# Down weights converted later, their loads behind an activation store, and a reordered, halved last token block

## The chip, the core and the metric

The kernel runs on one core of a Trainium2 chip. The metric is the device time of one execution in microseconds (us); lower is better. Five executions of the kernel before gave 632.99 to 637.2 us, median 633.97.

## What is computed

Linear attention with decay (4 batches, 8 heads, 768 tokens of 64 values, blocks of 64 tokens with a carried state), then a feed-forward block on its output. With `x` the attention output, 3072 tokens x 512:

```python
h = x @ w_in                      # 512 x 2048
g = np.maximum(0.01 * h, h)
out = g @ w_out                   # 2048 x 512, float32
```

`w_in` and `w_out` arrive as 64-bit floats, so each weight has to be turned into 32 bits on the chip. All products are wanted at nearly full float32 precision.

## The kernel before

The 3072 tokens are 24 chunks of 128 (`NCH`), in 6 groups of 4 chunks (`NG`, `GC`; 512 tokens a group). The 2048 hidden columns are 8 pieces of 256 (`NP`). The work has three parts that overlap.

*Attention*, one round for each chunk (`round_of`): transposes of k and q (L319), small 64x64 products (L274) into the PSUM tiles `po` and `psc`, and copies and products on VectorE, ScalarE and GpSimd. A round's last products (`inter(1)`) wait until a tiny copy has read `po` (L402). Each round also issues the loads of q, k (L299) and v (L304) for the chunk after the next. Its result is split in three reduced-precision parts: `xh` (L418), `xl` (L419), `xm` (L421).

*Up* (`up(g, p)`): for a group g and piece p, two halves of 128 hidden columns. Each half is three products of four 128x512 matmuls (L544): xh*wh and xl*wl summed in `b10` or `b11`, and xm*wm in `b2`. ScalarE evacuates the first sum to `t` (L565), VectorE joins it with `b2` in `gs` (L569), ScalarE applies the leaky ReLU (Prelu, L571), and SP stores the 512 KB to a DRAM tile `g` (L574). A step takes 24 matmuls.

*Down* (`down_load`, `down(g, p)`): SP loads `g` back (L584), ScalarE and VectorE split it in three (L591 to L594), and TensorE multiplies with the three parts of the down weights (L607). For every token block `tb` of 128 tokens there are two accumulators, `acc[tb][0]` for the h and l products and `acc[tb][1]` for the m products ("summed differences"). For tb = 3 both lie in the one PSUM tile `po`, for tb = 2 in `psc`; the other blocks have two separate tiles. After the last piece ScalarE reads `acc[tb][0]` into `t` (L616), VectorE joins it with `acc[tb][1]` (L618), and SP stores 256 KB of output (L621).

*Weights.* `to_float32` turns half a piece from 64 to 32 bits: SP loads 512 KB to one of two `raw` buffers (L470 for up, L473 for down weights), ScalarE does three operations (L482, L484, L486), VectorE two (L488, L489). For the down weights, `w_out(p)` does both halves and SP stores the result, 512 KB, in a DRAM tile `wo` (L523), because the space in which down weights end up is still taken by attention. Later `w_out_parts(p)` loads it (L527) and splits it in three.

*Order.* No order is written by hand. A list `seq` gives the pieces of work in rank; the `Plan` books each operation on an engine with a cost in us and emits the operation that can start first by its own clock; rank only breaks ties. A DMA is booked as busy for its cost, and what needs it may start 2.0 us later. Every engine then runs its own list strictly in the order in which the plan emitted it, SP's DMA issues among them. An operation without reads may go as soon as its buffer is free: the raw loads (`add("DMA", 1.6, load, [], ...)`) are such, so they may be emitted long before the place of their piece in `seq`. In `seq` a conversion `("wo", n_out)` follows every second step of the up work of groups 2 to 5, from step 0 on:

```python
        if n_out < NP and n % 2 == 0:
            seq.append(("wo", n_out))
            n_out += 1
```

Of the kernel before, what the change touches and what calls it, by code (L numbers as in the profile page):

```python
# [15 lines left out]
ALU = mybir.AluOpType  # L16
# [12 lines left out]
WS = S * U  # L29
# [7 lines left out]
class Plan:  # L37
# [20 lines left out]
    def add(self, eng, us, fn, reads=(), writes=(), rank=0.0):  # L58

        n, deps = len(self.ops), set()  # L60
        for k in reads:
            w, r = self.last.setdefault(k, [None, []])
            if w is not None:
                deps.add(w)
            r.append(n)
        for k in writes:
            w, r = self.last.setdefault(k, [None, []])
            if w is not None:
                deps.add(w)
            deps.update(r)  # L70
            self.last[k] = [n, []]
        deps.discard(n)
        ways = {eng: us} if isinstance(eng, str) else dict(zip(eng, us))
        if self.chain is not None:
            self.chains[self.chain].append(n)
        self.ops.append((ways, fn, deps, (self.rank + rank, n), set(writes)))
# [76 lines left out]
def kernel(  # L153
# [10 lines left out]
    nc = tc.nc  # L164
# [5 lines left out]
    d_model, d_ff = moe_w_in.shape  # L170
    KO = d_model // P
    NP = d_ff // (2 * P)
    NCH = B * NCB
    GC = 4
    NG = NCH // GC
# [12 lines left out]
    def sb(shape, name, dt=F32):  # L188
        return pool.tile(shape, dt, name=name, tag=name)
# [12 lines left out]
    raw = [sb([P, 2 * d_model], f"raw{i}") for i in range(2)]  # L202
    lows = [sb([P, d_model], f"low{i}", I32) for i in range(2)]
    w32 = sb([P, 2, d_model], "w32")
    tt = [sb([P, T], f"t{i}") for i in range(2)]
    gs = [sb([P, 2, T], f"gs{i}") for i in range(2)]
    WO = [dram.tile([P, 2 * d_model], F32, name=f"wo{p}", tag=f"wo{p}") for p in range(NP)]
    G = [[dram.tile([P, 2 * T], F32, name=f"g{g}_{p}", tag=f"g{g}_{p}") for p in range(NP)] for g in range(NG)]
# [38 lines left out]
    add = plan.add  # L247
# [209 lines left out]
    w_in_r = moe_w_in.rearrange("(ko ki) n -> ki ko n", ki=P)  # L457
    n_raw = 0

    def to_float32(kind, p, h, dst, key):  # L460

        nonlocal n_raw
        j, n_raw = n_raw % 2, n_raw + 1
        r, low, kl = raw[j], lows[j], f"low{j}"
        d = dst.bitcast(I32)

        def load():
            r64 = r.bitcast(I64)
            if kind == "wi":
                nc.sync.dma_start(out=r64.rearrange("p (k f) -> p k f", k=2),  # L470
                                  in_=w_in_r[:, 2 * h:2 * h + 2, p * 2 * P:(p + 1) * 2 * P])
            else:
                nc.sync.dma_start(out=r64, in_=moe_w_out[(2 * p + h) * P:(2 * p + h + 1) * P, :])  # L473

        def words(i, dt):
            return r.bitcast(dt).rearrange("p (n two) -> p n two", two=2)[:, :, i]

        def addend(dt, i):
            return low.bitcast(dt).rearrange("p (n two) -> p n two", two=2)[:, :, i]

        add("DMA", 1.6, load, [], [f"raw{j}"])
        add("ACT", 0.67, lambda: nc.scalar.activation(out=dst, in_=words(1, F32), func=AF.Abs, scale=2.0 ** -110),  # L482
            [f"raw{j}"], [key])
        add("ACT", 0.78, lambda: nc.scalar.activation(out=addend(U16, 0), in_=words(0, U32), func=AF.Copy, bias=0.0, scale=2.0 ** -29),  # L484
            [f"raw{j}"], [kl])
        add("ACT", 0.77, lambda: nc.scalar.activation(out=addend(F16, 1), in_=words(1, F32), func=AF.Copy, bias=0.0, scale=2.0 ** -100),  # L486
            [f"raw{j}"], [kl])
        add("DVE", 0.42, lambda: nc.vector.tensor_scalar(d, d, 3, None, op0=ALU.logical_shift_left), [], [key])  # L488
        add("DVE", 1.0, lambda: nc.vector.tensor_tensor(d, d, low, op=ALU.add), [kl], [key])  # L489
# [21 lines left out]
    def w_in(p):  # L511
        for h in range(2):
            to_float32("wi", p, h, w32[:, h, :], f"w32{h}")
        parts(p, w32f, ["w320", "w321"])

    ATT = ["fk", "fq", "sc"] + [f"{x}{i}" for x in ("k", "q", "v", "kT", "qT", "qsT") for i in range(2)] + [f"st{i}" for i in range(4)]
    NR = 4
    graw = [att[:, j * 2 * T:(j + 1) * 2 * T] for j in range(NR)]

    def w_out(p):  # L520
        for h in range(2):
            to_float32("wo", p, h, w32[:, h, :], f"w32{h}")
        add("DMA", 1.5, lambda: nc.sync.dma_start(out=WO[p], in_=w32f), ["w320", "w321"], [f"WO{p}"])  # L523

    def w_out_parts(p):
        j = p % NR
        add("DMA", 1.5, lambda: nc.sync.dma_start(out=graw[j], in_=WO[p]), [f"WO{p}"], [f"gr{j}"], rank=-3.0)  # L527
        parts(p, graw[j], [f"gr{j}"])
# [5 lines left out]
    def up(g, p, half=None):  # L534
# [42 lines left out]
    acc = [[b1[0], b2], [b1[1], pt.rearrange("p y t -> p (y t)")]] + [  # L577
        [z[:, i].rearrange("p y t -> p (y t)") for i in range(2)] for z in (psc, po)]
    ACC = [["b10", "b2"], ["b11", "pt"], ["psc", "psc"], ["po", "po"]]
# [17 lines left out]
    def down(g, p):  # L597

        nonlocal n_t
        for tb in range(GC):  # L600
            for pp in (p, p + 1):
                j = (g * NP + pp) % NR

                def go(tb=tb, pp=pp, j=j):
                    for f in range(2):
                        for z in range(3):
                            nc.tensor.matmul(acc[tb][z // 2], lhsT=ring[j][z][:, f * T + tb * P:f * T + (tb + 1) * P],  # L607
                                             rhs=W[pp][z][:, f * d_model:(f + 1) * d_model],
                                             start=pp == 0 and f == 0 and z != 1, stop=pp == NP - 1 and f == 1,
                                             skip_group_check=True)  # L610

                add("PE", 1.36, go, [f"r{z}{j}" for z in "hlm"] + [f"w{z}{pp}" for z in "hlm"], sorted(set(ACC[tb])))
            if p + 2 == NP:
                jt, n_t = n_t % 2, n_t + 1
                t, y = tt[jt], gs[jt][:, 0, :]
                add("ACT", 0.6, lambda t=t, tb=tb: nc.scalar.activation(out=t, in_=acc[tb][0], func=AF.Copy, bias=0.0, scale=(1.0 + 1.0 / S) / U),  # L616
                    [ACC[tb][0]], [f"t{jt}"], rank=-1.5)
                add("DVE", 0.69, lambda t=t, y=y, tb=tb: nc.vector.scalar_tensor_tensor(y, acc[tb][1], -1.0 / WS, t, op0=ALU.mult, op1=ALU.add),  # L618
                    [f"t{jt}", ACC[tb][1]], [f"gs{jt}"], rank=-1.5)
                rows = out[(g * GC + tb) * P:(g * GC + tb + 1) * P, :]  # L620
                add("DMA", 0.8, lambda rows=rows, y=y: nc.sync.dma_start(out=rows, in_=y), [f"gs{jt}"], [], rank=-1.5)  # L621

# [3 lines left out]
    seq = [("a", 0), ("wi", 0), ("a", 1), ("a", 2), ("up", 0, 0, 0), ("a", 3), ("wi", 1), ("up", 0, 1, 0), ("b", 4),  # L626
# [4 lines left out]
    nxt, n_out = 3 * GC, 0  # L631
    steps = [(g, p) for g in range(2, NG) for p in range(NP)]
    for n, (g, p) in enumerate(steps):
        while nxt < (g + 1) * GC:
            seq.append(("r", nxt))
            nxt += 1
        seq.append(("up", g, p))
        if nxt < NCH and nxt // GC < g + 2:
            seq.append(("r", nxt))
            nxt += 1  # L640
        if n_out < NP and n % 2 == 0:
            seq.append(("wo", n_out))
            n_out += 1
        if g == NG - 1:
            seq.append(("wp", p))
# [5 lines left out]
    for n, x in enumerate(seq):  # L651
        plan.rank = float(n)
        if x[0] in "abr":
            {"a": alone, "b": begun, "r": round_of}[x[0]](x[1])
        elif x[0] == "wi":
            w_in(x[1])
        elif x[0] == "up":
            up(*x[1:])
        elif x[0] == "wo":
            w_out(x[1])  # L660
        elif x[0] == "wp":
            if not freed:
                add("DVE", 0.0, lambda: None, [], ATT + [f"gr{j}" for j in range(NR)])
                freed = True
            w_out_parts(x[1])
        elif x[0] == "dl":
            plan.rank = n - 8.0
            down_load(*x[1:])
        else:
            down(*x[1:])  # L670
# [31 lines left out]
```

## Time and profile before

| | |
|---|---|
| profiled execution | 633.97 us |
| its span, first to last instruction | 632.2 us |
| median of five executions | 633.97 us |
| TensorE busy (PE) | 615.3 us |
| VectorE (DVE) / ScalarE (ACT) / GpSimd (POOL) busy | 350.4 / 277.9 / 80.4 us |
| mean granted TensorE clock | 0.996 |
| raw loads of down weights, first and last start | 95.6 and 186.3 us |
| raw loads of down weights, issue to landing | 3.5 to 6.0 us |
| store of a converted down weight, median to landing | 3.9 us |
| first and last load of a converted down weight (L527) | 293.9 and 344.8 us |

PE is TensorE's matmul side, PEld its weight loads. A line such as "PE po L274 <- issue: 3.5, 2, 2.0" in a list of waits gives the engine, the tile and line of the instruction that waited, what ended the wait, the total, the number of waits and the longest (us); "issue" means that the profile shows nothing the engine waited for. In a list in order of time a line gives start, duration, engine, line, operation, output and inputs, shape and count, and in brackets the idle time before it with what ended it. In a table of stretches each row gives start and end, length, the busy time of PE, PEld, DVE, ACT and POOL, the granted TensorE clock, the mean busy share of the 16 DMA engines, and GB/s.

### The profile page before, as it was taken

How to read it: one execution, taken by the hardware profiler on the slowest of the kernel's cores; microseconds unless marked ns; L12 is line 12 of the kernel's file. 1: busy time of each engine (PE TensorE's matmuls, PEld its weight loads, DVE VectorE, ACT ScalarE, POOL GpSimd, SP SyncE). 2: the span in 40 equal slices, each digit the busy share in tenths (PEclk: the TensorE clock that was granted, in tenths of full speed). 3: DMA queues.
4: the chain of work that ended last, by engine and by line, in shares of the span. 5: the costliest groups of instructions: out<-in, count | busy, mean ns of one | idle time of the engine just before them, and what ended most of it. 6: DMA issues, size and time to landing. Idle time of an engine off the chain costs nothing.

```text
span 632.2 us, 13360 instructions
## 1 busy us (share of the span) xinstructions
PE 615.3 (97%) x5587; PEld 515.0 (81%) x5587; DVE 350.4 (55%) x475; ACT 277.9 (44%) x403; POOL 80.4 (13%) x91
## 2 busy tenths in 40 slices
PE   7899999999989999999999999999999999999997
PEld 6787888887868888888888888888888888888885
DVE  5987986565754245245348866553735554545531
ACT  5687778766656444443344442312312222313111
POOL 3443500232331123021000000000000000000000
PEclk9999999999989999999999999999999999999999
DMA  7978857796986356233525663341432423343201
GB/s 194 248 213 213 242 198 252 265 261 219 268 240 203 107 144 169 100 102 119 200 117 185 219 212 134 116 150 67 160 108 101 167 87 132 116 132 116 85 0 67
DMA packets 103693, 101.54 MB, mean 161 GB/s; under 512 B 78545, under 2 KB 80593, under 8 KB 103633
## 3 DMA queue, kind: packets, MB, share of 16 engines
q1 hardware_dynamic: 103488, 100.68, 50.2%
q8 instruction: 44, 0.72, 0.5%
q14 instruction: 17, 0.13, 0.1%
q10 hardware_dynamic: 144, 0.00, 0.0%
HBM read 65.02 MB, written 35.65 MB: 159 GB/s over the span
## 4 chain that ended last, share of the span: by engine, by line
PE 89%; DMA 4%; DVE 2%; issue 2%; ACT 1%; SPq 1%; ACTq 0%
PE b L544 39%; PE b L607 17%; PE po L607 10%; PE psc L607 10%; PE po L274 4%; PE pt L607 3%; PE psc L274 3%; DMA raw<-in_moe_w_in_dram 3%; PE po L319 1%; PE pt L319 1%; SPq L299 1%; DMA att<-in_v_dram 1%; DMA att<-g 1%; DVE gs L569 0%; DVE xl L419 0%
## 5 line engine op out<-in xcount | busy, mean ns | idle before, releaser
L569 DVE SCALAR_TENSOR_TENSOR gs<-b,t 128x512 f32<-128x512 f32 x96 | 66.1, 689 | 90.7 <-PE b L544 72.2
L591 ACT ACTIVATE xh<-att 128x1024 fp32r<-128x1024 f32 x48 | 50.9, 1061 | 141.8 <-PE po L607 138.3
L592 DVE SCALAR_TENSOR_TENSOR xl<-att,xh 128x1024 fp32r<-128x1024 f32 x48 | 58.7, 1222 | 95.7 <-ACT xh L591 95.6
L544 PE MATMUL b<-xh,wh 128*128 128x512 f32 (+1 forms) x416 | 107.5, 380 | 1.1 <-ACT xh L418 0.8
L544 PE MATMUL b<-xl,wl 128*128 128x512 f32 (+1 forms) x416 | 105.6, 376 | 0.5 <-DVE wl L500 0.5
L544 PE MATMUL b<-xm,wm 128*128 128x512 f32 (+1 forms) x416 | 104.8, 376 | 0.8 <-DVE gs L569 0.6
L565 ACT ACTIVATE t<-b 128x512 f32<-128x512 f32 x96 | 57.0, 594 | 70.4 <-PE b L544 69.8
L544 PEld LDWEIGHTS b<-xl,wl 128*128 128x128 f32 x416 | 75.2, 189 | 14.9 <-DVE wl L500 0.7
L544 PEld LDWEIGHTS b<-xh,wh 128*128 128x128 f32 x416 | 74.2, 189 | 16.0 <-ACT xh L418 1.2
L544 PEld LDWEIGHTS b<-xm,wm 128*128 128x128 f32 x416 | 73.8, 188 | 15.7 <-DVE gs L569 1.4
L607 PE MATMUL b<-wh,xh 128*128 128x512 f32 x192 | 74.8, 390 | 0.1
L607 PE MATMUL b<-wl,xl 128*128 128x512 f32 x192 | 74.7, 389 | 0.0
L571 ACT ACTIVATE gs<-gs 128x1024 f32<-128x1024 f32 (+1 forms) x52 | 51.6, 992 | 41.4 <-DVE gs L569 41.0
L594 DVE SCALAR_TENSOR_TENSOR xm<-xl,xh 128x1024 fp32r<-128x1024 f32 x48 | 58.7, 1225 | 4.6
L332 POOL TENSOR_TENSOR att<-att 128x512 f32<-128x512 f32 (+1 forms) x24 | 26.2, 1092 | 143.4 <-PE po L319 131.7
L607 PEld LDWEIGHTS b<-wh,xh 128*128 128x128 f32 x192 | 36.1, 188 | 8.0 <-ACT t L565 0.5
L607 PEld LDWEIGHTS b<-wl,xl 128*128 128x128 f32 x192 | 36.1, 188 | 7.3
L274 PE MATMUL po<-att 64*64 64x64 f32 x1472 | 33.6, 222 | 4.1 <-issue 3.5
L607 PE MATMUL pt<-wm,xm 128*128 128x512 f32 x96 | 37.4, 389 | 0.0
L607 PE MATMUL psc<-wh,xh 128*128 128x512 f32 x96 | 37.3, 389 | 0.0
L607 PE MATMUL psc<-wl,xl 128*128 128x512 f32 x96 | 37.3, 389 | 0.0
L607 PE MATMUL psc<-wm,xm 128*128 128x512 f32 x96 | 37.3, 389 | 0.0
(69 smaller groups left out, 818.4 us busy)
## 6 DMA issues: line engine op xcount, KB each, us to landing
att<-g SPq DMA_DIRECT2D x48, 512.0 KB, 3.2
g<-gs SPq DMA_DIRECT2D x44, 512.0 KB, 3.0
raw<-in_moe_w_in_dram SPq DMA_DIRECT2D x16, 512.0 KB, 4.8
raw<-in_moe_w_out_dram SPq DMA_DIRECT2D x16, 512.0 KB, 4.5
att<-in_k_dram SPq DMA_DIRECT2D x48, 128.0 KB, 4.2
att<-in_q_dram SPq DMA_DIRECT2D x48, 128.0 KB, 3.6
att<-in_v_dram SPq DMA_DIRECT2D x24, 256.0 KB, 4.5
out_dram<-gs SPq DMA_DIRECT2D x24, 256.0 KB, 2.1
```

The source lines that it names most:

```text
L274: nc.tensor.matmul(dst[HALF[cols]], lhsT=lhsT[HALF[rows]], rhs=rhs[HALF[rows]], start=start, stop=True, skip_group_check=True)
L299: nc.sync.dma_start(out=dst[:, z * HP:(z + 1) * HP, :], in_=y[z::2].rearrange("h p d -> p h d"))
L319: nc.tensor.transpose(out=at[y], in_=src[:, 2 * y:2 * y + 2, :].rearrange("p a d -> p (a d)"), identity=ident)
L332: add("POOL", 1.15, lambda: nc.gpsimd.tensor_tensor(kr[nr], kr[nr], _bc(pow_k, 3, D)[nr], op=ALU.mult), ["fk"], [f"k{i}"])
L544: nc.tensor.matmul(dst, lhsT=w[z][:, kk * 2 * P + f * P:kk * 2 * P + (f + 1) * P], rhs=x[z][:, kk, toks], start=start and kk == 0, stop=kk ...
L565: add("ACT", 0.6, lambda t=t, b=b: nc.scalar.activation(out=t, in_=b, func=AF.Copy, bias=0.0, scale=(1.0 + 1.0 / S) / U), [kb], [f"t{jt}"] ...
L569: add("DVE", 0.69, lambda t=t, r=r: nc.vector.scalar_tensor_tensor(r, b2, -1.0 / WS, t, op0=ALU.mult, op1=ALU.add), [f"t{jt}", "b2"], [f"g ...
L571: add("ACT", 1.05 if half is None else 0.6, lambda: nc.scalar.activation(out=y, in_=y, func=AF.Prelu, bias=0.0, scale=1.0, alpha=0.01), [] ...
L591: add("ACT", 1.05, lambda: nc.scalar.activation(out=h, in_=graw[j], func=AF.Copy, bias=0.0, scale=NEAR), reads, wr("h"))
L592: add("DVE", 1.25, lambda: nc.vector.scalar_tensor_tensor(l, graw[j], 1.0, h.bitcast(F32), op0=ALU.mult, op1=ALU.subtract), reads + [f"rh{ ...
L594: add("DVE", 1.25, lambda: nc.vector.scalar_tensor_tensor(m, l.bitcast(F32), -S, h.bitcast(F32), op0=ALU.mult, op1=ALU.add), [f"rh{j}", f" ...
L607: nc.tensor.matmul(acc[tb][z // 2], lhsT=ring[j][z][:, f * T + tb * P:f * T + (tb + 1) * P], rhs=W[pp][z][:, f * d_model:(f + 1) * d_model ...
```

## The change

Two edits to the down weights' conversion. It starts after step 4 of the up work of group 2 and later instead of step 0 (still every second step, eight in all), and its raw loads now read the key of the activation store of the step before (`G` of that group and piece), so that they can't be issued before that store has landed. And an edit to the last token block of the kernel (group 5, tb = 3): the 8 matmuls of h and l of both last pieces come first, then the 4 of m, instead of h, l, m in turn; the joining operation on VectorE and the output store are done in two halves of 256 columns. All other token blocks keep their order; the PE operations are only booked in the plan with costs written in another way.

```diff
-    def to_float32(kind, p, h, dst, key):
+    def to_float32(kind, p, h, dst, key, after=()):
...
-        add("DMA", 1.6, load, [], [f"raw{j}"])
+        add("DMA", 1.6, load, after, [f"raw{j}"])
...
-    def w_out(p):
+    def w_out(p, after):
         for h in range(2):
-            to_float32("wo", p, h, w32[:, h, :], f"w32{h}")
+            to_float32("wo", p, h, w32[:, h, :], f"w32{h}", after)
...
+            done = p + 2 == NP
+            very_last = done and g == NG - 1 and tb == GC - 1
...
+            for pps, zs in (((p, p + 1), (0, 1)), ((p, p + 1), (2,))) if very_last else (((p,), (0, 1, 2)), ((p + 1,), (0, 1, 2))):
+                add("PE", 0.227 * 2 * len(pps) * len(zs), lambda pps=pps, zs=zs, go=go: go(pps, zs),
+                    needs(pps, ["hlm"[z] for z in zs]), sorted({ACC[tb][z // 2] for z in zs}))
...
-                add("DVE", 0.69, lambda t=t, y=y, tb=tb: nc.vector.scalar_tensor_tensor(y, acc[tb][1], -1.0 / WS, t, op0=ALU.mult, op1=ALU.add),
-                    [f"t{jt}", ACC[tb][1]], [f"gs{jt}"], rank=-1.5)
...
-                add("DMA", 0.8, lambda rows=rows, y=y: nc.sync.dma_start(out=rows, in_=y), [f"gs{jt}"], [], rank=-1.5)
+                n = 2 if very_last else 1
+                for i in range(n):
+                    cols = slice(i * d_model // n, (i + 1) * d_model // n)
+                    add("DVE", 0.69 / n + 0.08 * (n - 1),
+                        lambda t=t, y=y, tb=tb, cols=cols: nc.vector.scalar_tensor_tensor(
+                            y[:, cols], acc[tb][1][:, cols], -1.0 / WS, t[:, cols], op0=ALU.mult, op1=ALU.add),
+                        [f"t{jt}", ACC[tb][1]], [f"gs{jt}{i}" if n == 2 else f"gs{jt}"], rank=-1.5)
+                    add("DMA", 0.8 / n, lambda rows=rows, y=y, cols=cols: nc.sync.dma_start(out=rows[:, cols], in_=y[:, cols]),
+                        [f"gs{jt}{i}" if n == 2 else f"gs{jt}"], [], rank=-1.5)
...
-        if n_out < NP and n % 2 == 0:
-            seq.append(("wo", n_out))
+        if n_out < NP and n >= 4 and n % 2 == 0:
+            seq.append(("wo", n_out, ["G%d%d" % steps[n - 1]]))
             n_out += 1
```

More of the change, by code (lines that the diff above doesn't have):

```diff
@@ L600, in down, with go @@
         for tb in range(GC):
-            for pp in (p, p + 1):
-                j = (g * NP + pp) % NR
-                def go(tb=tb, pp=pp, j=j):
+            done = p + 2 == NP
+            very_last = done and g == NG - 1 and tb == GC - 1
+            def go(pps, zs, tb=tb):
+                for pp in pps:
+                    j = (g * NP + pp) % NR
                     for f in range(2):
-                        for z in range(3):
+                        for z in zs:
                             nc.tensor.matmul(acc[tb][z // 2], lhsT=ring[j][z][:, f * T + tb * P:f * T + (tb + 1) * P],
@@ L610, in go, with needs @@
                                              skip_group_check=True)
-                add("PE", 1.36, go, [f"r{z}{j}" for z in "hlm"] + [f"w{z}{pp}" for z in "hlm"], sorted(set(ACC[tb])))
-            if p + 2 == NP:
+            def needs(pps, zs):
+                return [f"{x}{z}{y}" for pp in pps for z in zs for x, y in (("r", (g * NP + pp) % NR), ("w", pp))]
+            for pps, zs in (((p, p + 1), (0, 1)), ((p, p + 1), (2,))) if very_last else (((p,), (0, 1, 2)), ((p + 1,), (0, 1, 2))):
+                add("PE", 0.227 * 2 * len(pps) * len(zs), lambda pps=pps, zs=zs, go=go: go(pps, zs),
+                    needs(pps, ["hlm"[z] for z in zs]), sorted({ACC[tb][z // 2] for z in zs}))
+            if done:
                 jt, n_t = n_t % 2, n_t + 1
@@ L659 @@
         elif x[0] == "wo":
-            w_out(x[1])
+            w_out(*x[1:])
         elif x[0] == "wp":
```

## Prediction

> **What bounds the kernel now.** I read the page first (busy shares, slices), then what TensorE waited for, then the busy time in stretches of 20 and of 2 us, then TensorE in order of time around its stalls, and the last 5 us.
>
> ```profile
> PE 615.3 (97%) x5587; PEld 515.0 (81%) x5587; DVE 350.4 (55%) x475; ACT 277.9 (44%) x403; POOL 80.4 (13%) x91
> q8 instruction: 44, 0.72, 0.5%
> ```
>
> TensorE is busy 615.3 of 632.2 us and has the same matmuls after the change, so only its 16.9 us of gaps, and time at a lower clock, can be won. The rows below are stretches: length, then busy PE, PEld, DVE, ACT, POOL, granted clock, DMA share, GB/s.
>
> ```profile
> 140.00:160.00 20.00, 18.45 (x306) 15.71 (x303) 11.49 (x19) 12.98 (x22) 4.75 (x6) 1.00 0.74 233
> 160.00:180.00 20.00, 17.88 (x320) 14.82 (x319) 12.42 (x22) 14.03 (x23) 7.12 (x8) 1.00 0.95 270
> 180.00:200.00 20.00, 19.54 (x203) 16.23 (x204) 9.94 (x19) 13.01 (x21) 6.05 (x7) 0.91 0.69 211
> ...
> 240.00:260.00 20.00, 20.00 (x212) 16.81 (x211) 8.20 (x15) 8.45 (x13) 4.49 (x6) 1.00 0.47 121
> ```
>
> From 80 to 140 us TensorE is full. In 140 to 200 it idles 1.55 + 2.12 + 0.46 = 4.13 us; from 200 to 300, where attention goes on and no down weight is converted, 0.04. Its waits in 138 to 186 us (total, times, longest):
>
> ```profile
> PE po L274 <- issue: 3.5, 2, 2.0
> PE b L544 <- DVE gs L569: 0.6, 1, 0.6
> ```
>
> The big one waits for nothing that the profile shows. TensorE in order of time, at both places:
>
> ```profile
> 141.52 0.28 PE L274 MATMUL po<-att 64*64 64x64 f32 x3
> 143.35 0.45 PE L274 MATMUL po<-att 64*64 64x64 f32 x13 [1.55 <-issue]
> ...
> 178.09 0.41 PE L274 MATMUL po<-att 64*64 64x64 f32 x13
> 180.47 0.42 PE L274 MATMUL po<-att 64*64 64x64 f32 x3 [1.97 <-issue]
> 180.82 2.08 PE L544 MATMUL b<-xh,wh 128*128 128x512 f32 x4
> 182.69 1.68 PE L544 MATMUL b<-xl,wl 128*128 128x512 f32 x4
> 184.21 0.62 PE L544 MATMUL b<-xm,wm 128*128 128x512 f32 x2
> ```
>
> Both stops are inside a group of 16 products (after 3, after 13), so no operand is missing: instructions are. Counting a weight load and a matmul for each record, the first stop is at instruction 4,289 of TensorE's program and the second at 5,314: 1,025 apart, four times 256 and one. After the second, 8 matmuls take 184.21 - 180.82 = 3.39 us instead of 8 x 0.2275 = 1.82: 1.57 us lost to the clock.
>
> ```profile
> 180.00:182.00 2.00, 1.53 (x6) 1.22 (x7) 0.00 (x0) 1.07 (x3) 0.96 (x1) 0.64 1.07 325
> 182.00:184.00 2.00, 2.00 (x7) 1.52 (x6) 1.71 (x3) 0.59 (x1) 1.04 (x3) 0.51 0.89 199
> ```
>
> [...] 0.72 MB in 44 packets is 16.4 KB each, 11,226 instructions / 256 = 43.9; [...] the stop of 1.55 us brought no drop. [...] Output stores of 256 KB land in 2.0 to 3.1 us (median 2.1)[...].
>
> **The change, part by part.**
>
> *Conversions leave 95 to 202 us.* Each of the eight has two loads and one store of 512 KB, on ScalarE 2 x (0.666 + 0.788 + 0.780) = 4.47 us, on VectorE 2 x (0.51 + 0.74) = 2.5 us. All go past SP's q, k, v loads and activation stores; GpSimd has none of it. TensorE's order stays up to the round at 139 us; later third products move by a place or two and rounds spread out from one per step to one per two steps. What goes: the stops, 1.55 + 1.97; the clock, 1.57; the wait on gs and its neighbour, 4.13 - 3.52 = 0.61. Sum 5.70 us.
> What hides fetches elsewhere is length: in steady matmuls a block lasts 128 x 0.2275 = 29 us. Only a block that lies wholly in an attention round is short. In before there are three: at 139 us (3.4 us by its durations), 176 us (2.5 us) and 283 us (2.7 us). The first two stopped: their next block came 5.4 and 4.5 us after they began. The third didn't, with a DMA share of 0.34. So a fetch takes under 2.7 us in quiet and 4.5 to 5.4 us in traffic. In after, by the order of its program: the block at 139 us is the same (traffic less by the store of w and two loads: I take 0.2 us, ends 0 and 1.5); the next has ten instructions of up matmuls in it, 2.9 us (I take 0); the one in the round of chunk 21, about 280 us, is now 2.1 us, and conversions run there: with a fetch of 3.3 us, between quiet and traffic, it stops 1.2 us (ends 0 and 3.2, and 1.57 for the clock).
>
> *They arrive at about 195 to 302 us.* From 200 to 300 ScalarE was busy 42.3 of 100 us, VectorE 41.3; plus 8 x 4.47 and 8 x 2.5 makes 78 and 61. DMA share there was 0.42 on average; 12.6 MB more in 100 us, by 419 GB/s at a share of 1.06 (138 to 140 us), adds 0.31: 0.73, below the 0.74 to 0.95 that hurt. Nothing saturates. Their last consumer, the load at L527 of the eighth weight at 344.8 us, comes 40 us later.
>
> *The wait.* Each pair of raw loads waits on SP for the landing of an activation store: 2.6 us in quiet, 5.3 at most there (200 to 300 us). Behind it on SP are q, k, v loads of the next round and the next store. That store is a step away, 24 x 0.2275 = 5.5 us, so it isn't late; q, k, v are late by up to 3 us, but rounds are now about 14 us apart, so nobody waits: 0. The raws land 3.5 (quiet) to 6.0 us after issue. The planner books 1.5 + 2.0 and 1.6 + 2.0 = 7.1 us for the two, reality takes 6.1 + 0.7 of issue in quiet. ScalarE and VectorE take the conversion in order; behind a late raw stand L565 (t), L402 (which lets a round's last products go) and L569 (which frees b2). Following the two programs with these durations against TensorE's products of 0.91 us, six of the eight conversions leave 0.2 to 1.8 us of slack; the one beside the round of chunk 21 leaves none, the last one misses by 0.5. The last, to show it: its raws are in ScalarE's reach 0.1 + 0.3 + 2.6 + 0.35 + 3.5 = 6.9 us after the Prelu of step (4, 1) ends; in ScalarE's order 4.47 of conversion, two evacuations (0.6 each), a Prelu (1.06) and an attention copy (0.6) follow before t of step (4, 4) is out, 14.2 in all; TensorE wants that buffer 15 products and two short groups, 13.7, later. I take 0.5 + 0.4 for raws that land later than in quiet, 0.9 us (ends 0 and 8 x 1.2).
>
> *The tail.*
>
> ```profile
> 627.78 0.60 ACT L616 ACTIVATE t<-po 128x512 f32<-128x512 f32 x1 [2.12 <-PE po L607]
> 628.41 0.69 DVE L618 SCALAR_TENSOR_TENSOR gs<-po,t 128x512 f32<-128x512 f32 x1 [2.03 <-ACT t L616]
> ```
>
> The summed products (h, l) now end four matmuls, 0.91 us, before the last; that could cover the 0.60 of the activation. But po is one tile with both sums, and in the program as built that activation still waits for the last matmul of po. So 0 (if it didn't: -0.6). The halves: 2 x 0.41 (the 128x256 row of L370 takes 0.41) instead of 0.69 ends VectorE 0.13 later; [...] the first half's issue, 0.34, fits beside the second. Net -0.1 (-0.3 to +0.2).
>
> **Sum.** The profiled execution took 633.97 us, 1.8 more than its span, and is also the median of the five (632.99 to 637.2). 633.97 - 5.70 = 628.27; + 0.2 + 1.2 + 0.9 - 0.1 = 630.5.
>
> **Rivals.**
> *Nothing new stops* (0.15): quiet fetches below 2.1 us and all slack holds: 628.2. For it: 0.04 us idle from 200 to 300 us; against: more traffic there.
> *The stop only moves* (0.28): the short block at 280 us meets full traffic (3.0 us, then the clock, 1.57), and the one at 139 us keeps 1.0: 628.27 + 3.0 + 1.57 + 1.0 + 0.9 - 0.1 = 634.6. For it: that block is the shortest of all; against: traffic of 0.73, not 0.95.
> *The waiting loads hold ScalarE up* (0.09, slower): one mechanism, at L482 behind the raw: if store and raw land as in traffic (5.3 + 6.0 instead of 6.1), the pair is 4 us over the booked 7.1, TensorE idles what exceeds some 1 us of slack, 8 x 1.5 = 12: 628.2 + 12 = 640. It decides from about 2.2 us over (8 x 1.2 = 9.6: 637.9). Against: G stores of 2.6 us in quiet.
> *The likeliest* (0.48): 630.5, its own range 629.0 to 632.0.
>
> **Numbers.** 0.5% is 3.2 us, about what a measurement of this kernel can tell from no change: faster is below 630.8. The likeliest case lies on that side with somewhat over two thirds: 0.15 + 0.35 = 0.50 faster; 0.41 same; 0.09 slower. Range 628.0 to 635.0: it leaves out the slow case and the upper third of the moving stop.
>
> **What would show it.** Right: no "issue" wait over 0.3 us and clock 1.00 in 120 to 200 us; PE 20.00 in those stretches; ScalarE near 0.78 in 200 to 300; one stop of TensorE near 280 us at most; the last activation still after the last matmul. Wrong: "issue" of over 1 us at 139 us (then its traffic was stores and q, k, v), waits of ScalarE on raw of over 1 us each with TensorE idle behind L565 or L402, or a tail shorter by 0.6.

## The result and the profile after

The changed kernel took 630.92 us (median of 22 runs, 627.2 to 635.24); the kernel before, run beside it, 634.07 us (43 runs, 630.75 to 637.95). The ratio is 0.9947, with a 95% interval of 0.9929 to 0.9965: about 3.4 us won, and somewhere between 2.2 and 4.5. The forecast of 630.5 us was met. Single runs of one kernel lie up to 8 us apart, more than the effect, so each trace below is one sample: the medians say how much, the traces say where.

The profiled execution of the changed kernel took 630.97 us, its span is 629.2 us. From its page, TensorE's share and the time in which the down weights' raw loads land (the last column):

```profile
PE 614.9 (98%) x5587; PEld 513.0 (82%) x5587; DVE 347.0 (55%) x474; ACT 274.6 (44%) x405; POOL 79.7 (13%) x91
raw<-in_moe_w_out_dram SPq DMA_DIRECT2D x16, 512.0 KB, 6.1
```

TensorE's idle time is 629.2 - 614.9 = 14.3 us; it was 16.9. The raw loads take 6.1 us in the median instead of 4.5. The same stretches of 20 us as before, and the 100 us to which the conversions moved:

```profile
120.00:140.00 20.00, 19.60 (x382) 16.90 (x374) 10.43 (x19) 9.38 (x16) 7.86 (x9) 1.00 0.66 169
140.00:160.00 20.00, 19.19 (x313) 16.22 (x312) 6.59 (x12) 8.19 (x14) 5.51 (x6) 1.00 0.40 114
160.00:180.00 20.00, 19.92 (x332) 16.53 (x331) 10.39 (x20) 7.97 (x14) 8.10 (x10) 1.00 0.63 163
180.00:200.00 20.00, 19.99 (x210) 16.66 (x209) 7.19 (x13) 9.49 (x16) 4.18 (x5) 1.00 0.58 177
200.00:300.00 100.00, 99.38 (x1298) 82.43 (x1297) 54.41 (x99) 68.32 (x111) 19.70 (x22) 1.00 0.71 230
```

Between 140 and 200 us TensorE idles 0.81 + 0.08 + 0.01 = 0.90 us, where it idled 4.13, and its clock stays at 1.00, where 180 to 200 us showed 0.91. The DMA share there fell from 0.74, 0.95 and 0.69 to 0.40, 0.63 and 0.58. The price is in the neighbouring rows: 0.40 us idle in 120 to 140 (none before) and 0.62 in 200 to 300 (0.04 before). What TensorE waited for from 80 us to the end (total, times, longest):

```profile
PE po L274 <- issue: 0.8, 1, 0.8
PE po L319 <- DMA att<-in_k_dram: 0.4, 1, 0.4
PE b L544 <- DVE gs L569: 0.3, 1, 0.3
PE po L274 <- DVE att L402: 0.3, 1, 0.3
```

One of the two stops that wait for nothing visible is left, and it is the one at the same place in the program. TensorE in order of time in the round at 139 us:

```profile
141.63 1.11 PE L274 MATMUL psc<-att 64*64 64x64 f32 x64
142.56 0.28 PE L274 MATMUL po<-att 64*64 64x64 f32 x3
143.65 0.45 PE L274 MATMUL po<-att 64*64 64x64 f32 x13 [0.81 <-issue]
```

After 3 products of a group of 16, as before: instruction 4,289 again. (In both traces 4,261 weight loads and matmuls come up to this place, and 28 instructions of TensorE's sequencer, semaphore waits for the most part, which no line of the lists shows. The prediction names only the weight loads and matmuls, but its 4,289 counts both.) The end of the kernel:

```profile
623.84 1.07 PE L609 MATMUL po<-wm,xm 128*128 128x512 f32 x4
624.95 0.60 ACT L624 ACTIVATE t<-po 128x512 f32<-128x512 f32 x1 [2.12 <-PE po L609]
625.58 0.76 DVE L631 SCALAR_TENSOR_TENSOR gs<-po,t 128x256 f32<-128x256 f32 x2 [2.03 <-ACT t L624]
```

The activation, which needs only the h and l sums, starts when all four m products have ended. From its start to the end of the span it takes 629.2 - 624.95 = 4.25 us; before, 632.2 - 627.78 = 4.42.

### The profile page after: what moved, and what is told of

It is laid out like the page before. It is cut to its first block, busy times and chain, and to the rows that moved or that the text cites. A ratio compares the mean times of both kernels' runs of the same rounds, so it can differ in the third digit from the quotient of the medians.

```text
span 629.2 us, 13356 instructions
## 1 busy us (share of the span) xinstructions
PE 614.9 (98%) x5587; PEld 513.0 (82%) x5587; DVE 347.0 (55%) x474; ACT 274.6 (44%) x405; POOL 79.7 (13%) x91
## 4 chain that ended last, share of the span: by engine, by line
PE 86%; DMA 8%; ACT 2%; DVE 2%; issue 1%; SPq 0%; DVEq 0%; ACTq 0%
PE b L544 35%; PE b L609 17%; PE po L609 10%; PE psc L609 10%; DMA raw<-in_moe_w_in_dram 5%; PE po L274 4%; PE pt L609 3%; PE psc L274 3%; DMA att<-in_k_dram 2%; PE po L319 2%; PE pt L319 1%; DMA raw<-in_moe_w_out_dram 1%; ACT w L482 1%; ACT low L486 1%; DVE w L488 0%
## 5 line engine op out<-in xcount | busy, mean ns | idle before, releaser
L592 DVE SCALAR_TENSOR_TENSOR xl<-att,xh 128x1024 fp32r<-128x1024 f32 x48 | 58.6, 1222 | 94.6 <-ACT xh L591 94.5
L569 DVE SCALAR_TENSOR_TENSOR gs<-b,t 128x512 f32<-128x512 f32 x96 | 66.1, 688 | 75.6 <-PE b L544 67.5
L544 PE MATMUL b<-xm,wm 128*128 128x512 f32 (+1 forms) x416 | 106.0, 379 | 0.5 <-DVE gs L569 0.3
L544 PE MATMUL b<-xl,wl 128*128 128x512 f32 (+1 forms) x416 | 105.3, 374 | 1.1 <-issue 0.6
L544 PE MATMUL b<-xh,wh 128*128 128x512 f32 (+1 forms) x416 | 105.6, 375 | 0.3 <-ACT xh L418 0.2
L544 PEld LDWEIGHTS b<-xh,wh 128*128 128x128 f32 x416 | 74.5, 188 | 15.5 <-ACT t L565 0.7
L544 PEld LDWEIGHTS b<-xl,wl 128*128 128x128 f32 x416 | 74.6, 188 | 14.7 <-DVE wl L500 0.7
L544 PEld LDWEIGHTS b<-xm,wm 128*128 128x128 f32 x416 | 73.1, 188 | 15.3 <-DVE gs L569 1.0
L565 ACT ACTIVATE t<-b 128x512 f32<-128x512 f32 x96 | 56.3, 590 | 51.2 <-PE b L544 45.0
L609 PE MATMUL po<-wh,xh 128*128 128x512 f32 x96 | 37.3, 389 | 0.0
L609 PE MATMUL po<-wl,xl 128*128 128x512 f32 x96 | 37.3, 389 | 0.0
```

What stands on the lines that cost most here:

```text
L544: nc.tensor.matmul(dst, lhsT=w[z][:, kk * 2 * P + f * P:kk * 2 * P + (f + 1) * P], rhs=x[z][:, kk, toks], start=start and kk == 0, stop=kk ...
L565: add("ACT", 0.6, lambda t=t, b=b: nc.scalar.activation(out=t, in_=b, func=AF.Copy, bias=0.0, scale=(1.0 + 1.0 / S) / U), [kb], [f"t{jt}"] ...
L569: add("DVE", 0.69, lambda t=t, r=r: nc.vector.scalar_tensor_tensor(r, b2, -1.0 / WS, t, op0=ALU.mult, op1=ALU.add), [f"t{jt}", "b2"], [f"g ...
L592: add("DVE", 1.25, lambda: nc.vector.scalar_tensor_tensor(l, graw[j], 1.0, h.bitcast(F32), op0=ALU.mult, op1=ALU.subtract), reads + [f"rh{ ...
```

## The experiments

Theory: TensorE's stops are blocks of instructions that arrive late because DMA traffic delays their fetch, and the change wins by taking the conversions' transfers away from the two short blocks. Rivals: (a) the conversions' work on ScalarE and VectorE, not their transfers, held TensorE; (b) what counts is only where a block's boundary falls, so that any shift of the program does the same; (c) the gain is the tail's. Every ratio is to the kernel before, measured beside it on the same chip; the kernel before took 633.54 us there (median) for the first four, 634.07 for the next four, 633.37 for the last three.

The first half of the theory can be read from the traces: they hold the transfers of the instruction queue (`q8 instruction` in the view of the DMA queues, 44 packets of 16 KiB), each with its time. One packet is one block: the trace of before has 11,224 instructions of TensorE and its sequencer, 255 to a packet. In order, around five stops of TensorE (us):

| kernel, instruction at the stop | the block ahead begins | packet, start to end | TensorE goes on |
|---|---|---|---|
| before, 4,289 | 137.93 | 141.07 to 142.01 | 143.35 |
| before, 5,314 | 175.99 | 178.15 to 179.09 | 180.47 |
| changed, 4,289 | 138.32 | 140.88 to 142.31 | 143.65 |
| experiment 7, 4,289 | 136.65 | 140.66 to 141.60 | 143.01 |
| experiment 8, 4,289 | 139.98 | 144.94 to 145.91 | 147.14 |

After 80 us, the traces of the changed kernel, the kernel before and the experiments have 17 stops of 0.3 us or more that wait for nothing visible. Each of them ends 1.2 to 1.6 us after such a packet has ended. So a stop is the wait for a block. The packet itself takes 0.9 to 1.6 us wherever it lies in the traces of before and of the changed kernel; what differs is how long after the start of the block ahead it begins, 2.2 to 5.0 us in the table. The experiments ask what makes it begin late.

### 1 and 2: the kernel before, with fillers that shift the blocks

```diff
-        add("PE", 0.44, lambda: go(tk, at), [f"k{i}"], [key])
+        add("PE", 0.44, lambda: (busy(12) if c == 3 else None, go(tk, at)), [f"k{i}"], [key])
```

12 filler products (24 instructions) ahead of chunk 3's transposes:

> The kernel before with 12 more filler transposes ahead of chunk 3's transposes, where TensorE waited 1.5 us for k: 24 more instructions ahead of all later work, so the fetch blocks fall elsewhere in the attention rounds; no traffic, no conversion and no order is changed. Theory F (TensorE stops because a whole fetch block lies in one attention round): the shortest blocks after 60 us are now 4.2, 4.2 and 4.0 us instead of 3.4 and 2.5, so no issue wait over 0.8 us near 139 and 176 us, and 634.1 - 3.5 - about 1 (clock) = 629.6, ends 628.5 to 631. Rival T (what hurts is the crowd of conversions on ScalarE, VectorE and the DMA engines itself, wherever blocks lie): same as before, 633.5 to 634.7.

Measured: 631.32 us, ratio 0.9968 (0.9951 to 0.9984): about half of what was expected. TensorE's stops in its trace, which is of an execution of 633.66 us, over two above the median:

```profile
139.02 0.64 PE L544 MATMUL b<-xm,wm 128*128 128x256 f32 x4 [1.03 <-issue]
145.76 0.35 PE L274 MATMUL psc<-att 64*64 64x64 f32 x9 [0.81 <-issue]
182.00 0.46 PE L274 MATMUL po<-att 64*64 64x64 f32 x15 [1.72 <-issue]
```

These are instructions 4,033, 4,289 and 5,314. The last two are the numbers at which the kernel before stopped, although other products stand there now: the stops keep to the count (4,289 - 4,033 = 256), not to the code. That is what blocks of 256 do. The block that began at 139.02 us was followed by the next only at 145.76, 6.7 us later. So from the start of a block to the arrival of the next 6.7 us can pass, more than the 5.4 that the prediction read from before. The expectation, which took 4.2 us for long enough, was wrong on the stops; that fits a gain of only half.

With 24 fillers (48 instructions):

```diff
-        add("PE", 0.44, lambda: go(tk, at), [f"k{i}"], [key])
+        add("PE", 0.44, lambda: (busy(24) if c == 3 else None, go(tk, at)), [f"k{i}"], [key])
```

> The kernel before with 24 more filler transposes at the same place (48 instructions). Theory F: blocks of 1.9 us near 68, 3.9 near 126, 3.1 near 166, 2.0 near 237 and 1.9 near 267 us; the first and third lie in traffic (DMA share 0.8 to 0.95), so stops move to about 68 and 166 us, 1 to 3 us each, and the time is 634 to 637. Rival T: same as before, 633.5 to 635.

Measured: 633.14 us, ratio 1.0007 (0.9981 to 1.0033), a little under the range that was expected. Its trace is of an execution of 637.19 us, again above the median:

```profile
137.67 0.49 PE L274 MATMUL po<-att 64*64 64x64 f32 x8 [2.39 <-issue]
183.56 0.39 PE L274 MATMUL psc<-att 64*64 64x64 f32 x10 [2.48 <-issue]
```

Another shift and no gain. The stops stand at instructions 4,033 and 5,314, two of the numbers of the first shift, and not at about 68 and 166 us, where they were expected. So (b) holds in part: where a boundary falls does change the time, by 0.3% in the first of the two and by nothing that shows in the second. The first can't be told from the changed kernel by its time (0.9968 against 0.9947, and 0.997 when that was measured again in 9). That the gain needs no shift is shown by 7, which moves no instruction of TensorE.

### 3 and 4: the parts of the change

The changed kernel with the wait left out (`[]` for its key). The planner then makes the same order of conversions as before, whether they may begin at step 0 or at step 4, so that the later start alone does nothing and this kernel is the one before with the new tail:

```diff
-        if n_out < NP and n >= 4 and n % 2 == 0:
-            seq.append(("wo", n_out, ["G%d%d" % steps[n - 1]]))
+        if n_out < NP and n % 2 == 0:
+            seq.append(("wo", n_out, []))
```

> The kernel after without the wait of the raw loads on the activation store. As built this has the order of the kernel before on every engine except in the last token block; it is the same program whether the conversion's place in the list is step 0 or step 4. So it is the tail edit alone. By the prediction: -0.1 us (-0.3 to +0.2), 634.0. Rival (the activation is covered by the last products): -0.6, 633.5; in the profile the last activation would start before the last matmul ends.

Measured: 633.8 us, ratio 0.9999 (0.9981 to 1.0016).

```profile
145.22 0.45 PE L274 MATMUL po<-att 64*64 64x64 f32 x13 [2.92 <-issue]
182.89 0.33 PE L274 MATMUL po<-att 64*64 64x64 f32 x3 [1.03 <-issue]
```

Both stops are back, at 4,289 and 5,314, after 3 and after 13 products of their groups, and the raw loads run from 94.6 to 187.2 us. What moves the conversions is the wait. The counterpart has the move without the new tail:

```diff
-            very_last = done and g == NG - 1 and tb == GC - 1
+            very_last = False
```

> The kernel after with the last token block as before: the moved and waiting conversions alone. By the prediction this is nearly the whole change: 631.0, ends 630 to 632. Rival (the tail edit gives 0.6 or more of the gain): 631.6 or more.

Measured: 630.44 us, ratio 0.9955 (0.9932 to 0.9977), with two stops of 0.5 us. The move is the whole gain within the intervals, and (c) falls.

### 5: the wait, from the first step on

```diff
-        if n_out < NP and n >= 4 and n % 2 == 0:
-            seq.append(("wo", n_out, ["G%d%d" % steps[n - 1]]))
+        if n_out < NP and n % 2 == 0:
+            seq.append(("wo", n_out, ["G%d%d" % steps[n - 1] if n else "G10"]))
```

> The kernel after with the conversions begun at step 0 again, but with the wait kept: each pair of loads waits for the store of the step before (the first for that of group 1, piece 0). The conversions then run from about 165 to 275 us, one per two steps. Theory F (traffic makes the fetch late, and pacing thins the traffic): the 139 us block is clear, the 176 us block meets the first conversions: a stop of 0 to 2 us; 631 to 632.5. Rival P (only the place away from the 176 us rounds matters): as before, 633.5 to 634.5. Rival W (the wait alone is all of it): as after, 630.5 to 631.

Measured: 628.88 us, ratio 0.9912 (0.9885 to 0.9938). TensorE's waits from 80 us to the end:

```profile
PE po L274 <- issue: 0.3, 1, 0.3
PE po L274 <- DVE att L402: 0.3, 1, 0.3
PE po L319 <- DMA att<-in_k_dram: 0.2, 1, 0.2
```

That is under all three times that were expected. The raw loads land in 5.4 us (median) instead of 6.1, and ScalarE waited 3.3 us for them instead of 7.0. Its interval just overlaps the changed kernel's, so a start at step 0 may be better than one at step 4; experiment 10 comes back to it.

### 6: the last block's two sums in two tiles

In the changed kernel both sums of the last token block lie in one tile (po). Token blocks 0 and 1 have them in two, so the last group of chunks is finished in the order 2, 3, 0, 1:

```diff
-        for tb in range(GC):
+        for tb in (2, 3, 0, 1) if p + 2 == NP and g == NG - 1 else range(GC):
-            very_last = done and g == NG - 1 and tb == GC - 1
+            very_last = done and g == NG - 1 and tb == 1
```

> The kernel after with the last token block's two sums in separate PSUM tiles: in the last down step the blocks go in the order 2, 3, 0, 1, and block 1 (sums in b11 and pt) gets the treatment of the last block. If the tail edit failed only because both sums lie in one tile, the last activation now starts about 0.9 us before the last matmul ends and the 0.60 us goes: after - 0.6, some 630.3. Rival (the activation is slowed by TensorE's writes, or the VectorE halves wait for something else): no change against after.

Measured: 629.42 us, ratio 0.9926 (0.9902 to 0.995). The end in its trace:

```profile
622.60 1.07 PE L609 MATMUL pt<-wm,xm 128*128 128x512 f32 x4
622.80 0.60 ACT L624 ACTIVATE t<-b 128x512 f32<-128x512 f32 x1 [1.44 <-PE b L609]
623.76 0.76 DVE L631 SCALAR_TENSOR_TENSOR gs<-pt,t 128x256 f32<-128x256 f32 x2 [1.68 <-PE pt L609]
```

Now the activation runs beside the m products, and VectorE waits for TensorE (pt), not for ScalarE. From the end of the last product (622.60 + 1.07 = 623.67) the span has 627.4 - 623.67 = 3.73 us to go; in the changed kernel 629.2 - (623.84 + 1.07) = 4.29. That is 0.56 us, the price that the prediction set for a tail that did what its order suggests. The time is 0.9 us under what was expected; the rest of the distance to the changed kernel is within the spread.

### 7: the kernel before, its down-weight loads cut to an eighth

ScalarE and VectorE keep every instruction and its size; the transfers shrink, and most of each buffer keeps old words, so that this kernel leaves out most of the down weights.

```diff
-                nc.sync.dma_start(out=r64, in_=moe_w_out[(2 * p + h) * P:(2 * p + h + 1) * P, :])
+                nc.sync.dma_start(out=r64[:, 0:64], in_=moe_w_out[(2 * p + h) * P:(2 * p + h + 1) * P, 0:64])
```

> The kernel before with each raw load of a down weight cut to an eighth (64 of 512 columns; the rest of the buffer keeps old words, so the down weights are not the reference's): 7.3 of 8.4 MB less traffic from 95 to 190 us, and the same work on ScalarE and VectorE at the same places. Theory F with traffic: fetches shorten to under 3.5 us, the stops at 139 and 176 us shrink to 0 to 1 us each, no clock drop: 629.5 to 631. Rival E (the crowd on ScalarE and VectorE is what costs): 633.5 to 634.5, with stops or waits as in before.

Measured: 630.88 us, ratio 0.9956 (0.9935 to 0.9978): the gain of the change, with the conversions where they were. A row of its stretches, and its one stop:

```profile
138.00:142.00 4.00, 2.50 (x121) 2.20 (x120) 1.71 (x3) 1.60 (x4) 1.06 (x1) 1.00 0.94 288
160.00:180.00 20.00, 20.00 (x333) 16.98 (x332) 12.88 (x24) 15.75 (x26) 8.52 (x10) 1.00 0.74 224
```

```profile
143.01 0.45 PE L274 MATMUL po<-att 64*64 64x64 f32 x13 [2.51 <-issue]
```

In 160 to 180 us ScalarE is busier than in before (15.75 us against 14.03) and TensorE is full; before, it idled 2.12 there. No instruction has moved, the stop at 5,314 is gone, and its packet ended at 175.88 us, 1.3 us before its block was due. So (a) falls as the cause of that stop: thinner traffic is enough to end it. The stop at 4,289 was expected to shrink and is even longer: in 138 to 142 us the share is still 0.94, and what moves then is q, k, v, stores of activations and of w.

### 8: the changed kernel, with traffic put back

18 loads of 512 KB into the idle raw buffers, read by nobody. They were meant for about 100 to 185 us and were issued from 115.9 to 201.1. (The lines that place them in `seq` are left out here.)

```diff
...
+        elif x[0] == "x":
+            add("DMA", 0.0, lambda i=x[1]: nc.sync.dma_start(out=raw[i % 2].bitcast(I64), in_=moe_w_out[i % 16 * P:(i % 16 + 1) * P, :]),
+                [f"gs{(n_g - 1) % 2}"], [f"raw{x[1] % 2}"])
```

> The kernel after with 18 more loads of 512 KB into the raw buffers while they lie idle (about 100 to 185 us), read by nobody; the order of every engine but SP is that of after. This puts the traffic of the old place back without its ScalarE and VectorE work. Theory F with traffic: stops return at 139 us (1.5 to 3 us) and 172 us (0 to 2 us), perhaps with a clock drop: 633 to 637. Rival E: 630.5 to 631.5, as after.

Measured: 647.96 us, ratio 1.0222 (1.0167 to 1.0278), far above what was expected. TensorE's waits from 80 to 330 us, and one stretch:

```profile
PE po L319 <- DMA att<-in_k_dram: 9.4, 5, 3.5
PE po L274 <- issue: 3.3, 1, 3.3
PE b L544 <- DVE gs L569: 1.2, 1, 1.2
```

```profile
140.00:160.00 20.00, 16.68 (x185) 13.63 (x184) 5.10 (x9) 6.18 (x11) 3.55 (x4) 0.83 0.71 213
```

The stop at 4,289 grew from 0.8 to 3.3 us, with a clock of 0.83: traffic alone, with no work on ScalarE or VectorE, lengthens it. The second stop, expected at 172 us, did not come back. The larger part of the loss is one that no theory had: TensorE waited 9.4 us for k, whose loads SP issues behind the extra ones. So this kernel shows the direction, and not the size, of what traffic does to fetches. For the stop at 5,314 it leaves something open: 7 shows that less traffic is enough to end it in the order of before, but in the changed kernel TensorE's order there is another too (the block ahead lasts 3.2 us instead of 2.5 without the stop), and no experiment parts the two.

### 9 to 11: the changed kernel again, and a better one

The changed kernel, unchanged:

> The kernel after unchanged, beside the two below on the same chip: 630.9, 0.993 to 0.997 of before. It tells whether the 2 us between it and the version with the wait from step 0 hold on one chip.

Measured: 631.25 us, ratio 0.997 (0.9948 to 0.9992). This second measurement of the change gives about 2 us instead of 3.4; the intervals overlap. Its trace has the stop at 4,289 again, 0.6 us, and waits of 0.6 and 0.4 for L569 and L565.

The edits of 5 and 6 together (no further edit):

> Both improvements found: the wait kept with conversions begun at step 0, and the last token block's sums in two tiles. If each is what it seemed (about -5 and -0.6 to before), 628.3; if the gain of step 0 was chance, 630.3.

Measured: 628.51 us, ratio 0.9921 (0.9895 to 0.9947).

```profile
PE po L274 <- issue: 0.9, 1, 0.9
PE po L319 <- DMA att<-in_k_dram: 0.7, 1, 0.7
PE b L544 <- DVE gs L569: 0.5, 1, 0.5
PE po L274 <- DVE att L402: 0.3, 1, 0.3
```

It beats the kernel before. It is 2.7 us lower in the median than the changed kernel measured beside it. The stop at 4,289 is still there, so the last kernel adds fillers of 112 instructions to it (28 small products), at the same place as in 1:

```diff
+        def shift():
+            for _ in range(28):
+                nc.tensor.matmul(b1[0][HALF[0]][:, 0:C2], lhsT=ident[HALF[0]][:, 0:C2],
+                                 rhs=ident[HALF[0]][:, 0:C2], start=True, stop=True, skip_group_check=True)
-        add("PE", 0.44, lambda: go(tk, at), [f"k{i}"], [key])
+        add("PE", 0.44, lambda: (shift() if c == 3 else None, go(tk, at)), [f"k{i}"], [key])
```

> The same with 28 more 64x64 filler products (112 instructions) where TensorE waits for k of chunk 3. By nominal durations the shortest fetch blocks are then 3.9, 3.2, 5.1 and 4.6 us (near 47, 101, 136, 141 us) instead of 3.4, 2.2 and 2.2 (near 119, 153, 253 us on the same scale). Theory F: 0.3 to 1 us less than the version without, with no issue wait after 130 us; if the traffic is by now thin enough to hide all fetches: the same.

Measured: 628.65 us, ratio 0.993 (0.9905 to 0.9955). In its trace (L549 is L544 of the others) no stop is left:

```profile
PE b L549 <- DVE gs L574: 1.1, 1, 1.1
PE po L319 <- DMA att<-in_k_dram: 1.1, 1, 1.1
PE po L274 <- DVE att L407: 0.3, 1, 0.3
```

and the median is that of 10. The stop went, waits for k and for L574 are longer by 0.4 and 0.6 us, and nothing is won. Whether a start at step 0 beats one at step 4 stays open: 10 (step 0) and 6 (step 4), both with the new tail, lie 0.9 us apart with intervals that cover each other.

## Why the prediction was right, point by point

The mechanism was right: late blocks of instructions (the packets of the instruction queue, and the fixed numbers of 1), made late by traffic (7 against rival (a), and 8). The traces of before and of the changed kernel show how far ahead a block is fetched. After 320 us, where a block lasts 29 us, the next packet begins 1.5 to 4.8 us before the block ahead does on TensorE, so that no more than one block is fetched ahead there. They show too that the packet doesn't begin at a fixed point of TensorE's own progress: after long matmuls it begins before the block ahead does (those 1.5 to 4.8 us), among attention products mostly after it (2.2 to 3.1 us at their three stops).

The sum came out within 0.5 us, but by errors that cancel, and so by luck: a stop that didn't come (+1.2) stands for busy time that nobody forecast (+1.17). Its terms against the trace (what before had and is gone is in the first row; what is new has its own):

| term | predicted, us | in the profiled execution, us |
|---|---|---|
| stops, clock, L569 wait of 140 to 200 us removed | -5.70 | -5.70 |
| block at 139 us | +0.2 | +1.21 (stop 0.81, wait for k 0.40) |
| block in the round of chunk 21 | +1.2 | 0 |
| late raw loads | +0.9 | +0.34 seen |
| tail | -0.1 | -0.17 |
| not predicted: short gaps | 0 | +0.21 |
| not predicted: TensorE busy for longer | 0 | +1.17 |
| sum | -3.5 | -2.94 (the two executions differ by 3.00) |

*The block at 139 us.* The failed step is "the same (traffic less by the store of w and two loads: I take 0.2 us". That block is 127 matmuls with their weight loads and two waiting instructions. Counted back in both traces, it begins with a matmul of L544 at 137.93 us in before and 138.32 in the changed kernel, and the next arrives at 143.35 and 143.65: 5.42 and 5.33 us. The fetch was hardly faster. The stop is 0.74 us shorter (0.81 instead of 1.55), and 0.40 of it is the wait for k, which the block now also holds and which hides as much of the fetch. Stretches of 2 us of the changed kernel show why:

```profile
138.00:140.00 2.00, 1.60 (x9) 1.01 (x7) 0.71 (x2) 1.12 (x2) 0.00 (x0) 1.00 1.12 354
140.00:142.00 2.00, 2.00 (x83) 1.76 (x85) 0.00 (x0) 0.71 (x2) 1.06 (x1) 1.00 0.53 169
...
280.00:282.00 2.00, 2.00 (x120) 1.83 (x122) 0.64 (x2) 2.00 (x5) 1.06 (x1) 1.00 0.03 10
```

In 138 to 140 us the share is 1.12 (1.06 before): loads of k and v and an activation store fill the engines just then. That the conversions left changes only what follows, 0.53 in 140 to 142 us instead of 0.94, and the packet began at 140.88 us instead of 141.07. The prediction had named this sign ("then its traffic was stores and q, k, v"), and 7, which kept the stop with raw traffic cut to an eighth, agrees. Which of these transfers holds the fetch up was not tried alone. 11 shows the exchange from the other side: without a stop, the waits for operands are longer.

*The block at 280 us.* The failed step is "with a fetch of 3.3 us, between quiet and traffic, it stops 1.2 us". The 0.73 of DMA share was right as a mean (0.71 over the 100 us), and TensorE is full in 280 to 282 us. What was wrong is the path: the prediction let the fetch begin with the block ahead. That block lies at 279.87 to 282.15 us, and the packet of the next ran from 278.29 to 279.23, before it began, behind long matmuls and in traffic (shares of 1.02 in 276 to 278 us and 0.76 in 278 to 280). The quiet of 280 to 282 us (0.03) came after it. A short block alone doesn't make a stop; the fetch has to begin late as well.

*The late raw loads.* They land in 4.5 to 7.0 us (median 6.1), not in 3.5 to 6.0: of the wait-then-load sequence the load was underrated. ScalarE did stand still for them:

```profile
ACT w L482 <- DMA raw<-in_moe_w_out_dram: 7.0, 4, 2.0
```

7.0 us in four waits, but TensorE shows only the 0.34 us behind L569 at 216 us. ScalarE had more slack than the prediction gave it, since its load was overstated: 78 us forecast in 200 to 300 us, 68.3 measured. The first conversion lies partly outside that stretch, but the main part is a misreading of durations. ScalarE in order of time (start, duration):

```profile
197.98 0.65 ACT L482 ACTIVATE w<-raw 128x512 f32<-128x512 f32 x1
198.52 0.78 ACT L484 ACTIVATE low<-raw 128x512 uint16<-128x512 uint32 x1
199.17 0.76 ACT L486 ACTIVATE low<-raw 128x512 f16<-128x512 f32 x1
199.80 0.64 ACT L482 ACTIVATE w<-raw 128x512 f32<-128x512 f32 x1
```

Each starts before the one ahead has ended. The three take 199.80 - 197.98 = 1.82 us from start to start, not 0.65 + 0.78 + 0.76 = 2.19. A conversion is 3.6 us of ScalarE, not 4.47, and 42.3 + 8 x 3.6 = 71 us, close to what was measured.

*TensorE busy for longer.* Before's 615.3 us held 1.57 of lower clock, so 613.7 was due; the trace shows 614.9. The three rows of L544 sum to 316.9 us against 317.9 - 1.57 = 316.3, which is half of it. The ends of matmuls are modelled, so a stall shorter than a group can pass for busy time; whether the rest is such stalls was not found. The kernel of experiment 5 has 613.7, so it isn't in the nature of the move.

*The tail.* As predicted: the activation waits for the last product of its tile (it starts at 624.95 us, the product ends at 624.91), and the halves win a little. The two half stores land 1.72 and 1.77 us after their issue, the whole stores ahead of them and those of before in 2.00 us or more; these two are all that shows it here. The -0.1 counted on half stores that land sooner, which no trace of before showed: it was the author's estimate. 3 shows that the whole is too little to measure, 6 what it takes to get the 0.56 us more.

*The rivals.* "Nothing new stops" was 2.8 us too low: TensorE idled 14.3 us and not 16.9 - 4.13 = 12.8, and the rest is busy time; "the stop only moves" did not come, for there is no stop at 280 us; "the waiting loads hold ScalarE up" was seen (7.0 us) but stayed under its cover.

*The signs.* Of those named for being right, three came: the clock of 1.00, a last activation after the last matmul, and at most one stop near 280 us (there is none); three did not: an "issue" wait is 0.81 us long, PE is busy 19.60 and 19.19 us of 20 in the two stretches from 120 to 160 us, and ScalarE is at 0.68 instead of 0.78. Of those named for being wrong, ScalarE's waits on raw came, 1.25 to 2.04 us each, with TensorE idle behind one of them. And the prediction's reading, that a fetch takes under 2.7 us in quiet and 4.5 to 5.4 us in traffic, is right in its effect only: the packet stays within the 0.9 to 1.6 us that it takes elsewhere, but begins late. How the traffic holds it back isn't shown.

## What to carry to other kernels

An idle engine that waits for "issue" inside a group of equal instructions may be waiting for its own program: count instructions between such stops, and if they are a multiple of 256 apart (here 256 and, but for one, 1,025), ask how long each block lasts, when the packet of the instruction queue begins, and what the DMA engines carry just before, not on average. Pacing bulk loads away from stretches of many small instructions can then win what the load of no engine explains (about 3.4 us here), and a test that shrinks the transfers but keeps the work (experiment 7) tells the two apart. For sums of ScalarE work in a row, take the distance from start to start, not the durations (here 1.82 us for three operations whose durations sum to 2.19).

## What the runs showed of the hardware that was not expected

- The late block is found at the same instruction number in every variant that has the stop there (4,289 in before, the changed kernel and experiments 1, 3, 4, 5, 7 to 10), though experiment 1 has 24 instructions more ahead of it.
- Of two stops of similar length one cost clock and one didn't: after the 2.51 us of experiment 7 the granted clock stayed at 1.00, after the 2.92 us of experiment 3 it was 0.61 and 0.54 in the next stretches of 2 us, and in before 1.97 us was enough. There the granted clock is 0.5 for 3.41 us, from 180.57 us on, longer than the stop ahead of it.
- A late block costs by the start of its packet and not by the length of it: 0.94 and 0.95 us of transfer behind the two stops of before, 0.96 us without a stop at 160 us, and after 80 us never less than 1.2 us from the end of a packet to the first instruction of its block.
